# Projection products per head step: from a fixed rate to a rate worked out from what is left

## The chip, the cores and the metric

The kernel runs on one NeuronCore of a Trainium2 chip. The metric is the device time of one execution in microseconds (us), lower is better. The engines that matter are TensorE (PE: matmuls; PEld: its weight loads), VectorE (DVE), ScalarE (ACT), GpSimd (POOL), and SyncE (SP), which here only issues DMAs.

## The reference

A network of four layers on one sequence of 2048 rows by 640 columns. Layers 1 and 3 are attention in a sliding window, layers 2 and 4 a Fourier mixing:

```python
x = A_x
x = x + _A_ref(_layernorm(x, axis=-1), A_wqkv, A_wo)
x = x + _B_ref(_layernorm(x, axis=-1), B_dft_seq_re, ...)
x = x + _A_ref(_layernorm(x, axis=-1), A_wqkv, A_wo)
x = x + _B_ref(_layernorm(x, axis=-1), B_dft_seq_re, ...)
# _A_ref: qkv = x @ wqkv; 32 heads of 20 columns; a row attends to itself and the
# 255 rows before it (mask, softmax); the heads' outputs @ wo
# _B_ref: a, b = x @ dft_hid_re.T, x @ dft_hid_im.T; y = dft_seq_re @ a - dft_seq_im @ b
```

All of it is float32. The kernel keeps that accuracy by splitting every factor into a high and a low part and making three products of each.

## The kernel before, in words

The sequence is cut into 16 blocks of 128 rows (and 4 blocks `sb` of 512), the 32 heads into 8 quads of four. Only the attention layers are touched by the change. Each of them has a head loop (`heads`), written in the order in which the engines will run it; nothing reorders it afterwards.

The loop goes over `step` from -10 to 128. A step handles one block of rows of one quad: step t = 16 * quad + block. It holds two halves (`z` is 0 or 1), and for each half TensorE makes two score tiles of the block that stands ten steps ahead (`s_head`, L631), from which VectorE takes masked row maxima (L636), and two transposed score tiles of the block at hand (`t_pair`, L659), which ScalarE turns into exponentials (L669) and GpSimd masks (L675, L679). At the end of the step stand the 12 times 4 products with the values (`pv`, L694). Every fourth step the maxima are turned into rows (`m_rows`, L644, L647) and sent by two small DMAs into an extra row of the queries (L649, `qp<-mt`), which the transposed score tiles four steps later read.

Beside the heads, three kinds of other work are laid into the steps, always right behind the first half (and behind the second one too in steps before -1):

- **The projection** of queries and keys (`project`, `pieces`, `lockstep`, L257): 600 products in all, 15 for each 128 columns (`c`, ten of them) and each `sb`. One product is two matmuls on the two halves of the rows. 120 are done before the loop. Two blocks `sb` make a piece of 30 products, in two halves of 15; at its end ScalarE copies two banks out (L544), GpSimd cuts them in two parts (L552, L211) and SP stores them (L524, `qk_d<-c`, 512 KB each). From there they come back in the layout of the heads (`pack`, L594, 80 KB each, twelve for one quad and one `sb`, three to a step).
- **The output's first part** (`partials`): 16 units of 18 products (three of the five chunks of the heads' outputs times `wo`), also on L257 with 320 columns. They need all 600 projection products done, the chunks loaded and scaled (`load_o`, L859, L865, L892), and the rows of x, which are loaded four ahead (`load_y`, L952, `big<-x`, 320 KB each; added in by VectorE on L978). `prepare(0)`, `prepare(2)` and `prepare(4)` start these loads when the projection comes to its last column block, to the second half of it, and to its end.
- **The output's last part** (`late`), from step 127.

How many products a step gets is `nf`. `fill(nf)` takes the half of 15 that is under way and cuts what is left of it into equal shares near `nf`. The deadlines `due` can raise `nf`; neither in this kernel nor in the changed one do they. With the fixed rate the steps from 0 on have 4, 4, 4 and 3 products in turn, steps -2 and -1 have 10 and 5, and the 600 are done at step 91. Steps 92 to 96 have no such product. The output's first part begins at step 97 with 9 products a step. SP issues all DMAs in program order, and each waits until the DMA eight places before it has landed, since there are eight completion semaphores in turn.

Of the kernel before, what the change touches and what calls it, by code (L numbers as in the profile page):

```python
# [31 lines left out]
EARLY = 3  # L32
AHEAD_X = 4
AFTER = 4
RATE = 4
FIRST = 7
LATE = 9
BACK = 2
# [26 lines left out]
class Net:  # L65
# [540 lines left out]
    def heads(self, xsrc, xdst, hook):  # L606
# [116 lines left out]
        total = NCH * NSB * per_piece  # L723
        done = [2 * NSB * per_piece]
# [52 lines left out]
        for step in range(-LEAD, steps + 1):  # L777
# [10 lines left out]
            s, t, v = step + LEAD, step, step - 1  # L788
# [8 lines left out]
            if v >= 0 and v % 4 == 3:  # L797
                load_v(v // 4 + 2)
            if done[0] < total:
                nf = max([FIRST if t < -2 else RATE + (t < 0)]  # L800
                         + [(d - done[0]) / max(1, at - s) for at, d, _, _ in due])
            else:
                nf = LATE
# [1062 lines left out]
```

## Time and profile before

| | us |
|---|---|
| median of 3 executions | 2182.82 |
| lowest, highest | 2181.66, 2192.8 |
| the profiled execution | 2187.93 |
| its span, first to last instruction | 2186.2 |
| steps 0 to 95 of the first attention (160.8 to 424.0) | 263.2 |
| steps 96 to 127 of the first attention (424.0 to 529.2) | 105.2 |
| steps 0 to 95 of the second attention (1252.1 to 1514.6) | 262.5 |
| steps 96 to 127 of the second attention (1514.6 to 1618.2) | 103.6 |

A step's start is the start of its first L659 matmul, of which there are four in a step. All times in the text count from the span's start. In the chain of waits a row has a start, a length, and the work that the end of the span hung on at that time; "x8" is eight instructions. In the table of stretches a row has the length and then for each engine its busy time and the number of its instructions, the granted TensorE clock (1.00 is full), the share of the DMA engines and GB/s.

### The profile page before, as it was taken

What the parts mean: (1) busy time and instruction counts of PE and PEld (TensorE: products, weight loads), DVE (VectorE), ACT (ScalarE), POOL (GpSimd) and SP (SyncE); (2) the same over time, 40 slices, a digit from 0 to 9 for tenths busy, and PEclk for the clock granted to TensorE, in tenths of its full rate; (3) what the DMA queues carried; (4) which work ended last, traced back from release to release, by engine and by line L of the source; (5) the groups of instructions that cost most, each with busy time, mean ns of one, the idle gap of its engine ahead of it and who ended that gap; (6) DMA issues with size and microseconds to landing.
All of it is one profiled execution on the core that took longest, in us unless ns stands there. A gap on an engine that the chain in (4) does not pass through costs nothing.

```text
span 2186.2 us, 48927 instructions
## 1 busy us (share of the span) xinstructions
PE 2118.1 (97%) x17872; PEld 1783.2 (82%) x17872; DVE 1603.7 (73%) x3931; ACT 1140.5 (52%) x2125; POOL 958.0 (44%) x1562
## 2 busy tenths in 40 slices
PE   7999999988999999999999999999899999999999
PEld 7987777677878888889999877776778888888899
DVE  6358888886897868786661588888767968677676
ACT  3117777656554545452341177777565645445332
POOL 3037776765614222322430377767655033231324
PEclk9999999999999999999999999999999999999999
DMA  5546666785555354656645556567855454546653
GB/s 183 175 157 190 198 180 215 211 224 169 202 192 189 127 183 141 214 177 207 207 156 167 162 186 200 181 212 226 216 161 182 140 182 132 174 152 208 222 165 125
DMA packets 227089, 398.40 MB, mean 182 GB/s; under 512 B 39969, under 2 KB 86561, under 8 KB 226849
## 3 DMA queue, kind: packets, MB, share of 16 engines
q1 hardware_dynamic: 226848, 395.28, 57.3%
q8 instruction: 141, 2.31, 0.5%
q14 instruction: 100, 0.81, 0.1%
HBM read 273.94 MB, written 120.06 MB: 180 GB/s over the span
## 4 chain that ended last, share of the span: by engine, by line
PE 78%; DVE 7%; DMA 5%; ACT 4%; issue 3%; POOL 2%; SPq 1%; ACTq 0%; DVEq 0%; POOLq 0%
PE banks L1416 29%; PE banks L239 15%; PE banks L257 12%; PE banks L694 6%; PE banks L659 5%; PE banks L1704 5%; PE banks L631 5%; DMA qp<-qk_d 2%; DVE banks L636 1%; ACT pt L669 1%; DMA x_d<-x 1%; PE banks L341 1%; DMA kp<-qk_d 1%; ACT big L1039 1%; DVE qp L232 1%
## 5 line engine op out<-in xcount | busy, mean ns | idle before, releaser
L636 DVE CUSTOM_DVE_ANT_0 banks<-banks,mask 128x384 f32<-128x384 f32 (+2 forms) x1024 | 527.6, 557 | 123.0 <-PE banks L631 99.9
L669 ACT ACTIVATE pt<-banks 128x768 f32<-128x768 f32 (+2 forms) x512 | 393.8, 772 | 168.7 <-PE banks L659 55.2
L675 POOL TENSOR_SCALAR_AFFINE_SELECT pt<-pt 128x256 f32<-128x256 f32 x512 | 213.3, 417 | 213.8 <-ACT pt L669 192.0
L257 PE MATMUL banks<-big,wc 64*128 64x512 f32 x1920 | 271.1, 394 | 0.4 <-DVE pt L442 0.4
L659 PE MATMUL banks<-qp,kp 61*128 61x384 f32 (+2 forms) x1024 | 210.2, 381 | 22.8 <-DVE mc L636 17.4
L694 PE MATMUL banks<-pt,vq 128*32 128x128 f32 x5760 | 211.6, 278 | 3.5 <-ACT pt L669 3.4
L631 PE MATMUL banks<-kp,qp 60*128 60x384 f32 (+2 forms) x1024 | 205.5, 347 | 6.7 <-DVE mc L636 3.1
L257 PEld LDWEIGHTS banks<-big,wc 64*128 64x128 f32 x1920 | 186.8, 185 | 22.6 <-ACT x L544 1.5
L679 POOL TENSOR_SCALAR_AFFINE_SELECT pt<-pt 128x256 f32<-128x256 f32 x448 | 193.8, 433 | 0.0
L226 ACT ACTIVATE qp<-pt 128x512 fp32r<-128x512 f32 (+1 forms) x200 | 123.2, 625 | 128.1 <-DVE pt L1347 51.7
L232 DVE TENSOR_TENSOR qp<-pt,qp 128x512 fp32r<-128x512 f32 (+1 forms) x198 | 156.6, 798 | 42.1 <-ACT qp L226 40.5
L694 PEld LDWEIGHTS banks<-pt,vq 128*32 128x32 f32 x5760 | 142.4, 110 | 51.5 <-issue 35.3
L659 PEld LDWEIGHTS banks<-qp,kp 61*128 61x128 f32 x1024 | 108.0, 184 | 87.3 <-DVE mc L636 65.2
L1416 PE MATMUL banks<-qp,big 128*128 128x512 f32 x648 | 152.9, 390 | 0.0
L631 PEld LDWEIGHTS banks<-kp,qp 60*128 60x128 f32 x1024 | 123.6, 186 | 31.9 <-DVE mc L636 16.4
L1345 POOL TENSOR_TENSOR pt<-pt,pt 128x512 f32<-128x512 f32 x32 | 47.2, 1475 | 231.4 <-DMA pt<-c 173.4
L226 ACT ACTIVATE c<-pt 128x512 fp32r<-128x512 f32 x146 | 90.4, 625 | 111.1 <-POOL pt L1325 57.1
L636 DVE DVE_READ_ACCUMULATOR2_ANT mc<- 128x1 f32 x1024 | 145.0, 142 | 0.0
L1416 PEld LDWEIGHTS banks<-qp,big 128*128 128x128 f32 x648 | 120.8, 188 | 24.2
L232 DVE TENSOR_TENSOR c<-pt,c 128x512 fp32r<-128x512 f32 x144 | 113.8, 793 | 26.9 <-ACT c L226 24.4
L1416 PE MATMUL banks<-qp,xc 128*128 128x512 f32 x480 | 117.4, 391 | 4.3 <-DVE xc L232 2.8
L552 POOL CAST c<-x 128x512 fp32r<-128x512 f32 x64 | 38.9, 611 | 166.5 <-ACT x L544 162.3
(253 smaller groups left out, 4479.9 us busy)
## 6 DMA issues: line engine op xcount, KB each, us to landing
pt<-c SPq DMA_DIRECT2D x166, 512.0 KB
qk_d<-c SPq DMA_DIRECT2D x80, 512.0 KB
kp<-qk_d SPq DMA_DIRECT2D x384, 80.0 KB
qp<-qk_d SPq DMA_DIRECT2D x384, 80.0 KB
kp<-u_d SPq DMA_DIRECT2D x32, 640.0 KB
o_d<-ou SPq DMA_DIRECT2D x64, 256.0 KB
x_d<-x SPq DMA_DIRECT2D x48, 320.0 KB
v_d<-pt SPq DMA_DIRECT2D x16, 768.0 KB
```

Source lines behind the costliest of these rows:

```text
L226: nc.scalar.activation(hi, src, AF.Copy, scale=-1.0 if neg else 1.0)
L232: (eng or nc.vector).tensor_tensor(out=lo, in0=src, in1=hi.bitcast(F32), op=OP.subtract)
L239: self.nc.tensor.matmul(p, x, y, start=n == 0, stop=n == last)
L257: self.nc.tensor.matmul(ps[a], x[r], y[r], start=half + i == 0, stop=half == 1 and i == n - 1, skip_group_check=True)
L631: nc.tensor.matmul(p, qp[quad % 2][b:b + 60, z, qb * P:(qb + 1) * P], kp[quad % 2][b:b + 60, z, k0 * P:(qb + 1) * P], start=True, stop=True)
L636: nc.vector.tensor_tensor_reduce(out=p, in0=p, in1=self.mask[:, 384 - n * P:], scale=1.0, scalar=NEG, op0=OP.add, op1=OP.max, accum_out=mc ...
L659: nc.tensor.matmul(self.banks[:, banks[e], :n * P], kp[quad % 2][b:b + 61, z, kb * P:(kb + 1) * P], qp[quad % 2][b:b + 61, z, kb * P:(kb + ...
L669: nc.scalar.activation(pt[quad, kb][:, 2 * z:2 * z + 2, :n * P], self.banks[:, b0:b1 + 1, :n * P], AF.Exp, scale=SCALE)
L675: nc.gpsimd.affine_select(out=t[:, :, 0:P], in_=t[:, :, 0:P], pattern=[[0, 2], [1, P]], compare_op=OP.is_ge, fill=0.0, base=0, channel_mul ...
L679: nc.gpsimd.affine_select(out=t[:, :, 256:384], in_=t[:, :, 256:384], pattern=[[0, 2], [-1, P]], compare_op=OP.is_gt, fill=0.0, base=0, ch ...
L694: nc.tensor.matmul(self.banks[32 * h:32 * h + 32, bank, :P], vq[:, 96 * (kb % 4) + 21 * h:96 * (kb % 4) + 21 * h + 32], t[:, h, (qb - kb) ...
L1416: nc.tensor.matmul(self.banks[:, bk, :], p, b[q], start=start and m == 0, stop=stop and last and m == 2, skip_group_check=True)
```

## The change

The constant 4 goes. From step -2 on, the number of products is what is left of the 600 divided by the number of steps left until step 96; in the steps before -2 it stays 7.

```diff
-RATE = 4
+ROWS_AT = 96
...
             if done[0] < total:
-                nf = max([FIRST if t < -2 else RATE + (t < 0)]
+                nf = max([FIRST if t < -2 else (total - done[0]) / max(1, ROWS_AT - t)]
                          + [(d - done[0]) / max(1, at - s) for at, d, _, _ in due])
             else:
                 nf = LATE
```

What comes of it: the rate is 3.67 at step -2 and falls slowly. Steps -2 and -1 have 8 and 4 products (10 and 5 before). From step 0 to 72 the shares are 3, 4, 4, 4 in turn, that is the old row one step later. Steps 73 to 77, 82 to 86 and 91 to 95 have 3 each, and the 600 are done at step 95. The output's first part begins at step 97 as before. In steps 0 to 91 nine products fewer are made than before, in steps -2 and -1 three fewer, and twelve stand in steps 92 to 95.

TensorE at step 92, before. The two score pairs of the step stand with nothing between them; `pt` holds the exponentials, `vq` the values:

```order
L659 MATMUL banks<-qp_105,kp_104 128x384 x2
L631 MATMUL banks<-kp_561,qp_106 128x384 x2
L659 MATMUL banks<-qp_105,kp_104 128x384 x2
L631 MATMUL banks<-kp_561,qp_106 128x384 x2
L694 MATMUL banks<-pt_96,vq_93 32x128 x4
```

The same step in the changed kernel; `big_512` and `big_732` hold two blocks of the normalized rows, `wc` the weights:

```order
L659 MATMUL banks<-qp_105,kp_104 128x384 x2
L631 MATMUL banks<-kp_561,qp_106 128x384 x2
L257 MATMUL banks<-big_512,wc 128x512
L257 MATMUL banks<-big_732,wc 128x512
L257 MATMUL banks<-big_512,wc 128x512
L257 MATMUL banks<-big_732,wc 128x512
L257 MATMUL banks<-big_512,wc 128x512
L257 MATMUL banks<-big_732,wc 128x512
L659 MATMUL banks<-qp_105,kp_104 128x384 x2
L631 MATMUL banks<-kp_561,qp_106 128x384 x2
L694 MATMUL banks<-pt_96,vq_93 32x128 x4
```

Three products, six matmuls, now stand between the halves of steps 92 to 95.

SP from step 92 to 96, before:

```order
L621 DMA vq_92<-v_d 128x384
L952 DMA big_5880<-x 128x640 x2
L594 DMA qp_106<-qk_d 20x2x512 x3
L524 DMA qk_d<-c 128x2x512
L711 DMA sm<-ou_99 128x1x16
L712 DMA o_d<-ou_99 128x512
L717 DMA r_d<-rc 128x16
L952 DMA big_5880<-x 128x640 x2
L524 DMA qk_d<-c 128x2x512
L649 DMA qp_106<-mt 2x4x128 x2
L594 DMA kp_104<-qk_d 20x2x512 x3
```

The same stretch in the changed kernel:

```order
L621 DMA vq_92<-v_d 128x384
L594 DMA qp_106<-qk_d 20x2x512 x3
L711 DMA sm<-ou_99 128x1x16
L712 DMA o_d<-ou_99 128x512
L717 DMA r_d<-rc 128x16
L649 DMA qp_106<-mt 2x4x128 x2
L594 DMA kp_104<-qk_d 20x2x512 x3
L621 DMA vq_93<-v_d 128x384
L952 DMA big_6021<-x 128x640 x2
L594 DMA kp_104<-qk_d 20x2x512 x3
L952 DMA big_6021<-x 128x640
```

Four loads of x rows and the two last stores of the projection no longer stand ahead of the small L649 of step 95; the first of the loads follow in step 96.

SP in steps 98 and 99, before:

```order
L717 DMA r_d<-rc 128x16
L594 DMA qp_105<-qk_d 20x2x512 x3
L859 DMA x<-o_d 128x1x512
L865 DMA rr_101<-r_d 128x1x512
L649 DMA qp_106<-mt 2x4x128 x2
L594 DMA qp_105<-qk_d 20x2x512 x3
L952 DMA big_5880<-x 128x640
```

The same two steps in the changed kernel:

```order
L717 DMA r_d<-rc 128x16
L952 DMA big_6021<-x 128x640
L594 DMA qp_105<-qk_d 20x2x512 x3
L859 DMA x<-o_d 128x1x512
L865 DMA rr_101<-r_d 128x1x512
L524 DMA qk_d<-c 128x2x512
L952 DMA big_6021<-x 128x640
L649 DMA qp_106<-mt 2x4x128 x2
L594 DMA qp_105<-qk_d 20x2x512 x3
L952 DMA big_6021<-x 128x640
L524 DMA qk_d<-c 128x2x512
```

Here two of the loads and one store have come in ahead of the L649 and the last L594 of step 99, and a store behind them.

## The prediction

> **What bounds the kernel now.** I read the page's engine shares first, then the table of stretches over the two attentions, then the chain of waits inside a stretch, and last SP's timeline.
>
> ```profile
> span 2186.2 us, 48927 instructions
> PE 2118.1 (97%) x17872; PEld 1783.2 (82%) x17872; DVE 1603.7 (73%) x3931; ACT 1140.5 (52%) x2125; POOL 958.0 (44%) x1562
> ```
>
> ```profile
> 160.80:424.00 263.20, 257.55 (x3620) 194.44 (x3618) 219.59 (x821) 190.71 (x349) 194.27 (x443) 1.00 0.64 196
> 424.00:529.20 105.20, 94.11 (x1442) 76.55 (x1442) 73.50 (x230) 64.59 (x117) 66.56 (x143) 0.98 0.72 204
> 1252.10:1514.60 262.50, 256.80 (x3624) 193.72 (x3620) 219.19 (x820) 190.77 (x349) 194.43 (x443) 1.00 0.63 199
> 1514.60:1618.20 103.60, 92.92 (x1442) 75.34 (x1442) 74.64 (x232) 64.79 (x117) 66.45 (x143) 1.00 0.73 197
> ```
>
> TensorE is busy for 98% of steps 0 to 95 and VectorE for 83%: TensorE leads, but VectorE is close behind. The two attentions differ by 0.7 us up to step 96 and by 1.6 us after it. The chain inside the plain part of the loop (steps 57 to 72 of the first attention):
>
> ```profile
> 313.85 0.37 PE banks L659
> ...
> 316.50 0.37 PE banks L659 x2
> 316.87 0.18 PE banks L631 x2
> 317.05 0.93 PE banks L257 x8
> 317.97 0.17 PE banks L659 x2
> 318.14 0.17 PE banks L631 x2
> 318.32 0.79 PE banks L694 x24
> ...
> 321.06 0.21 PE banks L644
> ...
> 322.06 0.37 PE banks L659 x2
> ...
> 322.61 0.70 PE banks L257 x6
> ...
> 324.66 0.37 PE banks L659 x2
> ...
> 333.16 0.26 PE banks L659 x2
> ...
> 335.60 0.38 PE banks L659 x2
> ...
> 343.47 0.37 PE banks L659 x2
> ...
> 346.04 0.37 PE banks L659 x2
> ...
> 354.69 0.38 PE banks L659 x2
> ...
> 357.28 0.37 PE banks L659 x2
> ```
>
> The step at 316.50 is pure TensorE: 0.37 + 0.18 + 0.93 + 0.17 + 0.17 + 0.79 = 2.61 us with four products. Four cost 0.93 and three 0.70, so a product costs 0.23 us of TensorE. Without products a step would need 1.68 us of TensorE, with three 2.38; every fourth step has the 0.21 of L644 on top. The four three-product steps in these rows (322.06 to 324.66, 333.16 to 335.60, 343.47 to 346.04, 354.69 to 357.28) last 2.60, 2.44, 2.57 and 2.59, on average 2.55, which is 0.17 above TensorE's own 2.38: something else holds them. All sixteen steps last 357.28 - 313.85 = 43.43; the twelve with four products take 33.23, or 2.77 each, and 2.70 without the L644 of four of them. So going from four products to three has been worth 0.15, not 0.23.
>
> **Where no product stands.** The chain in steps 92 to 95, and in the table of stretches step 95, step 96 and the same four steps of the second attention:
>
> ```profile
> 413.00 0.37 PE banks L659 x2
> ...
> 413.60 0.56 DVE banks L636
> ...
> 420.88 0.26 PE banks L659 x2
> ...
> 424.07 0.62 PE banks L659 x2
> ...
> 428.09 3.85 DMA qp<-mt
> ```
>
> ```profile
> 420.88:424.07 3.19, 2.86 (x35) 1.84 (x34) 2.46 (x10) 1.14 (x4) 2.12 (x4) 0.72 0.99 349
> 424.07:427.86 3.79, 3.39 (x35) 2.11 (x34) 2.81 (x10) 2.20 (x4) 2.01 (x4) 0.50 0.66 206
> 1504.30:1514.60 10.30, 9.07 (x135) 6.00 (x131) 9.13 (x34) 6.36 (x15) 9.99 (x22) 1.00 0.79 251
> ```
>
> Steps 92 to 94 (413.00 to 420.88) last 2.63 each on average though TensorE needs about 1.68: the chain runs through VectorE's mask (0.56), behind which the next score pair waits. In the second attention the four steps last 10.30, or 2.58 each. So a step costs about 2.6 whether it holds no product or three, and TensorE has some 0.7 us of room for products in each of these four.
>
> **The change, part by part**, for one attention.
>
> *A. Three products fewer in steps -2 and -1.* Five products took 1.15 there, and at step 0 VectorE is behind:
>
> ```profile
> 156.55 1.15 PE banks L257 x10
> ...
> 161.61 0.46 DVE banks L636
> 162.07 0.06 DVE mc L636
> ```
>
> Three at 0.23 are 0.7 us at most. But in step 0 the chain passes to VectorE, where a mask costs 0.46 + 0.06 = 0.52 in a row; a half with two masks and their start is near the half with four products (0.18 + 0.93), so TensorE soon waits for VectorE. Ends: -0.7 and 0. I take -0.5, nearer to the TensorE row, since only step 0 shows the wait.
>
> *B. Steps 0 to 91: nine steps go from four products to three.* Ends: 9 x 0.23 = -2.1 if TensorE alone counts, 0 if a step's floor is 2.7 already. I take the difference seen in the quoted steps, 9 x 0.15 = -1.4. Up to step 72 the row 4, 4, 4, 3 is only moved by one step against the heads' own work. ScalarE's copies at the end of a piece still fall into a step of three products, as before, so I cost the shift at nothing; what hides it is that light step. If that cover were gone, a copy more or less in the way would be a few tenths in each of eleven pieces, 1 to 2 us either way.
>
> *C. Steps 92 to 95: twelve products come in.* With three, TensorE needs 2.38 (2.59 with L644 in step 94); the three-product steps seen last 2.55. Four of them with L644 once, and shorter score tiles in the last two, come to 10.2 to 10.4, against 10.30 in the second attention: 0. Ends: +2.8 (12 x 0.23, nothing hidden) and -0.4 (if the wait for the mask disappears behind the products). In the steps from 96 on the last two bank copies, the GpSimd cuts and the two stores come later by four steps; these steps hold nine products, and ScalarE is busy there for 64.79 of 103.60 and GpSimd for 66.45, so I cost their engine time at nothing.
>
> *D. The clock.* In the first attention the granted clock falls to 0.72 in step 95 and 0.50 in step 96, at the end of the steps without products. In the second it stays at 1.00. By the first table this attention loses 0.7 up to step 96 and 1.6 behind it, together 2.3. With products in steps 92 to 95 I expect no fall: -2 in this execution, ends -2.3 and 0. Whether the executions behind the median had the fall isn't shown, so I count half of it there, -1. The page "TensorE: Matmul & The Clock Gate" of the Trainium skill says, under "HAM oscillation — how this bites in real kernels", that TensorE falls to half clock after idle gaps over about 3.4 us. By that rule these steps, with gaps under 1 us, should not have lost the clock, and the sum would be without this term, 1 us higher. The row of 0.50 differs from the page, and the row decides.
>
> *E. SP and the DMAs around steps 95 to 102.* SP's timeline and, last, the chain in the second attention:
>
> ```profile
> 1514.37 0.80 SPq L952 DMA_DIRECT2D big<-x_d  x2
> 1515.27 0.38 SPq L524 DMA_DIRECT2D qk_d<-c  x1
> ...
> 1517.45 1.19 SPq L594 DMA_DIRECT2D kp<-qk_d  x3
> ...
> 1531.11 1.26 SPq L594 DMA_DIRECT2D qp<-qk_d  x3
> ```
>
> ```profile
> 1532.02 4.17 DMA qp<-qk_d
> ```
>
> Step 102 begins quad 7's scores and can't start before the last L594 of step 99 has landed, at 1536.19, 21.6 us after step 96 began. Between 1517.45 and the last issue of that group at 1532.02 SP issues 24 DMAs, 0.6 us each, without a pause worth naming. In the changed kernel SP reaches step 96 earlier, since two loads and a store (1514.37 to 1515.65, some 1.3 us, and the waits around them) are gone from ahead of it; but five more stand between there and step 99's last L594: 5 x 0.6 = 3.0. Net +1.7 on SP, and by bytes (4 x 0.32 + 0.5 = 1.8 MB at the 251 GB/s of the row quoted above is 7.2 us, less the 1.15 MB, 4.6 us, of two loads and a store that were in flight at 1515 anyway) +2.6. Against it the L649 of step 95 is freed of the loads ahead of it: the 3.85 us wait of the first attention shrinks. Ends: -1.3 and +5. I take +1.0 an attention.
>
> The sum: A -0.5, B -1.4, C 0, E +1.0 make -0.9 an attention, -1.8 for both, and D -2: -3.8 from the profiled execution's own 2187.9, that is 2184.1. The median of the runs stands 5.1 below that execution, so from 2182.8, with half of D, 2182.8 - 2.8 = 2180.0.
>
> **The rivals.**
>
> *R1, slower: the loads in a bunch hold up SP.* Each DMA waits for the one eight places back. Six loads of x rows (four moved, two that were there) and two stores now stand in steps 96 to 99. For it: SP has no room there, and the one L524 issued at 1515.27 is of the kind that lands late under load. Against it: the bytes up to step 102 are the same. Its price: the upper end of E, 5 us an attention, instead of +1: 2180 + 8 = 2188, and 2192 if A and B give nothing as well. It decides where the first load of x rows, issued in the second half of step 96, lands later than VectorE needs it, which is at the end of step 98, some 8 us on: then L978 blocks the masks behind it.
>
> *R2, faster: TensorE alone counts.* A and B in full, -2.8 an attention, C -0.4, E -1.3 because the waits at steps 97 and 98 go: -4.5, twice, and -2 for the clock: 2182.8 - 11 = 2172. For it: 98% busy, and the step of 2.61 that is pure TensorE. Against it: three-product steps have not come below 2.44.
>
> *R3, nothing: the floor of the step.* If a three-product step in a run of them lasts as long as a four-product one, A to E cancel and only the clock may differ: 2182, between 2181 and 2184. For it: 2.6 with none and 2.55 with three.
>
> *R4: the clock falls elsewhere.* If the wait at step 102 grows by 1 us, TensorE idles over 5 us there, and a fall as in D costs 2.3 an attention: 2180 + 4.6 = 2185. For it: the fall in the first attention. Against it: the 4.17 us wait left the second attention's stretch at 1.00. [...]
>
> **How the numbers follow.** Forecast 0.42 (2176 to 2183), R3 0.22, R1 0.16, R2 0.14, R4 0.06. The predicted time is the forecast's, 2180. Range: down to 2170, just below R2's 2172, and up to 2193, R1 with nothing from A and B; what is left out is the tails of R1 and R2, about 0.15. 0.5% is 10.9 us, about what a measurement of this kernel can tell from no change: faster means under 2171.9, slower above 2193.7. R2 lies at the lower bound and gives 0.12 with a tail of the forecast; R1 reaches the upper with its tail, and with an alignment of steps 0 to 72 worse by 0.06 a step (6 us an attention), 0.14. The rest, 0.74, is within.
>
> **What would show it.** Right: steps 92 to 95 at 10.2 to 10.4 us with six L257 matmuls each and a clock of 1.00; steps 0 to 91 shorter by 1 to 2 us an attention; three-product steps at about 2.55; the DMA wait at step 102 a little longer, the wait for qp<-mt near step 97 gone. Wrong: a mean step other than 2.7 in steps 0 to 72 (the shift is not free), L978 waiting for big<-x at step 98, or SP late by more than 3 us at step 99.

## The result and the profile after

The changed kernel takes 2182.91 us in the median of 20 executions (2178.11 to 2187.48), the kernel before, run beside it, 2188.73 in the median of 20 (2181.66 to 2195.65). The ratio over the executions is 0.9981, with a 95% interval of 0.9972 to 0.9989, which is about 4 us; the two medians are 5.8 us apart. So the changed kernel is 4 to 6 us faster, a fifth to a quarter of a per cent. The 2182.82 shown before the prediction was the median of three executions and stood at the low end of the twenty.

The page of the changed kernel, its span and the engine shares, and its table of stretches: the two attentions (steps 0 to 95, then 96 to 127), steps 0 to 72 and 73 to 91 of the first, steps 92 to 95 of both, and 3 us inside step 102. Columns as before: length, then busy time of TensorE, weight loads, VectorE, ScalarE and GpSimd, granted clock, DMA share, GB/s.

```profile
span 2183.4 us, 48970 instructions
PE 2119.3 (97%) x17872; PEld 1785.2 (82%) x17872; DVE 1602.8 (73%) x3931; ACT 1139.6 (52%) x2125; POOL 961.1 (44%) x1562
...
159.70:419.60 259.90, 256.65 (x3628) 195.26 (x3624) 220.18 (x821) 190.41 (x349) 191.16 (x438) 1.00 0.65 197
419.60:525.80 106.20, 94.27 (x1442) 76.70 (x1439) 73.78 (x232) 64.80 (x118) 70.39 (x150) 0.98 0.71 206
1246.90:1507.00 260.10, 256.85 (x3628) 195.07 (x3625) 220.18 (x821) 190.38 (x349) 191.15 (x438) 1.00 0.64 197
1507.00:1615.40 108.40, 96.76 (x1442) 78.21 (x1442) 74.25 (x232) 64.89 (x118) 70.45 (x150) 0.96 0.72 197
...
159.72:356.88 197.16, 194.84 (x2758) 149.46 (x2757) 166.16 (x625) 144.23 (x263) 143.32 (x333) 1.00 0.64 195
356.88:408.45 51.57, 50.66 (x720) 37.84 (x717) 44.42 (x163) 38.34 (x69) 37.87 (x86) 1.00 0.68 209
408.40:419.60 11.20, 11.17 (x159) 7.95 (x153) 9.63 (x35) 7.85 (x17) 10.00 (x21) 1.00 0.72 198
1495.70:1507.00 11.30, 11.27 (x160) 8.00 (x155) 9.68 (x35) 7.90 (x17) 10.05 (x21) 1.00 0.60 179
442.10:445.10 3.00, 2.96 (x22) 2.96 (x23) 0.36 (x2) 0.00 (x0) 0.83 (x2) 0.50 0.77 260
```

The same view of the kernel before, for steps 0 to 72 and 73 to 91 of the first attention:

```profile
160.79:359.86 199.07, 195.66 (x2760) 148.77 (x2758) 164.94 (x624) 144.44 (x263) 142.66 (x331) 1.00 0.63 194
359.86:412.93 53.07, 52.06 (x735) 39.27 (x731) 45.05 (x164) 39.80 (x74) 41.56 (x91) 1.00 0.66 203
```

Steps 0 to 95 became shorter by 3.3 and 2.4 us (263.2 to 259.9, 262.5 to 260.1), steps 96 to 127 longer by 1.0 and 4.8. Of the gain in the first attention, 1.9 us lie in steps 0 to 72, which hold one product fewer (two matmuls in the counts), and 1.5 in steps 73 to 91, which hold eight fewer. Steps 92 to 95 cost 11.2 us in both attentions.

The chain of waits through steps 98 to 103 of the first attention, after the change (start, length, what the end hung on):

```profile
427.86 0.81 DVE big L978
...
436.53 0.44 SPq L594
437.02 0.36 SPq L594
437.42 4.68 DMA qp<-qk_d
442.14 0.47 PE banks L631
442.61 2.51 PE banks L257 x18
...
447.04 1.33 PE banks L257 x18
```

The wait that ended the chain at step 102 before ends it still: the last L594 lands at 442.10, 22.5 us after step 96 began. Right behind it 18 matmuls take 2.51 us, and the same 18 in the next step 1.33: the granted clock was 0.50 in those 3 us, as the last stretch above shows. The second attention has the same fall at the same place.

For all kernels of this case the stretches, from the starts of the steps in each profiled execution, first / second attention, in us ("lead" is the first L631 of the head loop to step 0):

| kernel | lead | 0-72 | 73-91 | 92-95 | 96-99 | 100-103 | 104-127 |
|---|---|---|---|---|---|---|---|
| before | 35.8 / 35.2 | 199.1 / 199.0 | 53.1 / 53.2 | 11.1 / 10.3 | 14.6 / 12.5 | 14.2 / 15.3 | 76.3 / 75.7 |
| after | 35.1 / 34.5 | 197.2 / 197.3 | 51.6 / 51.6 | 11.2 / 11.2 | 12.7 / 12.7 | 17.5 / 17.5 | 76.1 / 78.3 |
| e1_shift | 35.1 / 34.5 | 197.1 / 197.3 | 52.1 / 52.1 | 10.3 / 10.6 | 13.5 / 11.9 | 16.3 / 19.5 | 76.5 / 76.5 |
| e2_tail | 35.8 / 35.2 | 199.1 / 198.9 | 51.3 / 51.1 | 11.2 / 11.3 | 12.6 / 12.6 | 15.7 / 19.6 | 82.7 / 76.9 |
| e3_light1 | 35.1 / 34.5 | 196.2 / 196.9 | 52.3 / 52.3 | 10.7 / 10.8 | 12.2 / 12.2 | 14.6 / 17.1 | 78.3 / 78.4 |
| e4_light2 | 37.1 / 36.4 | 197.6 / 197.8 | 53.3 / 53.3 | 10.2 / 10.3 | 13.9 / 15.7 | 13.1 / 13.1 | 76.2 / 78.2 |
| e5_rows92 | 35.2 / 34.5 | 197.3 / 196.9 | 52.3 / 52.3 | 10.5 / 10.5 | 12.6 / 12.8 | 18.8 / 18.9 | 76.9 / 78.5 |
| e6_ahead2 | 35.1 / 34.5 | 197.0 / 197.8 | 51.6 / 51.5 | 11.3 / 11.2 | 12.6 / 12.6 | 13.9 / 16.1 | 77.6 / 75.7 |
| e7_pack_early | 35.1 / 34.5 | 197.2 / 197.2 | 51.5 / 51.6 | 11.2 / 11.2 | 13.0 / 13.5 | 14.7 / 13.7 | 79.9 / 75.9 |
| e8_early_light1 | 37.3 / 36.7 | 198.3 / 198.0 | 53.2 / 53.1 | 10.3 / 10.3 | 12.6 / 13.2 | 13.7 / 14.5 | 76.9 / 75.8 |
| e9_cut1 | 35.8 / 35.2 | 197.1 / 197.2 | 53.1 / 53.2 | 11.0 / 10.3 | 13.9 / 13.4 | 13.8 / 16.5 | 77.4 / 75.8 |
| e10_cutback | 35.1 / 34.5 | 197.4 / 197.7 | 51.7 / 51.7 | 11.2 / 11.2 | 12.7 / 12.6 | 17.9 / 19.0 | 76.4 / 75.8 |
| e11_both | 35.1 / 34.5 | 197.1 / 197.1 | 51.6 / 51.5 | 11.2 / 11.2 | 15.8 / 12.6 | 13.1 / 13.0 | 78.8 / 78.4 |
| e12_light1_both | 35.1 / 34.5 | 196.1 / 196.2 | 52.3 / 52.5 | 10.7 / 10.7 | 14.4 / 12.1 | 12.9 / 12.9 | 76.6 / 76.8 |

The columns up to step 95 repeat between the two attentions of an execution within 0.8 us, most within 0.3. Those behind it scatter by 1 to 6 us, since a fall of the clock there comes in one execution and not in the next. So the experiments are read by their stretches first, and by their times where several executions were taken. The letters that name theories in the expectations hold within a group of runs.

### The profile page after: what moved, and what is told of

The parts are those of the page before. It is cut to its first block, busy times and chain, and to the rows that moved or that the text cites. A ratio compares the mean times of both kernels' runs of the same rounds, so it can differ in the third digit from the quotient of the medians.

```text
span 2183.4 us, 48970 instructions
## 1 busy us (share of the span) xinstructions
PE 2119.3 (97%) x17872; PEld 1785.2 (82%) x17872; DVE 1602.8 (73%) x3931; ACT 1139.6 (52%) x2125; POOL 961.1 (44%) x1562
## 4 chain that ended last, share of the span: by engine, by line
PE 79%; DVE 7%; DMA 5%; ACT 4%; issue 3%; POOL 2%; SPq 1%; ACTq 0%; DVEq 0%; POOLq 0%
PE banks L1416 29%; PE banks L239 14%; PE banks L257 13%; PE banks L694 7%; PE banks L659 6%; PE banks L631 5%; PE banks L1704 5%; DVE banks L636 1%; DMA kp<-qk_d 1%; DMA kp<-u_d 1%; DVE qp L232 1%; ACT pt L669 1%; PE banks L341 1%; ACT big L1039 1%; POOL rs L1087 1%
## 5 line engine op out<-in xcount | busy, mean ns | idle before, releaser
L636 DVE CUSTOM_DVE_ANT_0 banks<-banks,mask 128x384 f32<-128x384 f32 (+2 forms) x1024 | 527.0, 556 | 116.7 <-PE banks L631 98.9
L659 PE MATMUL banks<-qp,kp 61*128 61x384 f32 (+2 forms) x1024 | 210.1, 380 | 21.5 <-DVE mc L636 16.4
L631 PE MATMUL banks<-kp,qp 60*128 60x384 f32 (+2 forms) x1024 | 210.2, 350 | 4.9 <-DMA qp<-qk_d 3.5
L226 ACT ACTIVATE qp<-pt 128x512 fp32r<-128x512 f32 (+1 forms) x200 | 123.2, 625 | 129.0 <-DVE pt L1347 52.1
L659 PEld LDWEIGHTS banks<-qp,kp 61*128 61x128 f32 x1024 | 108.4, 185 | 85.3 <-DVE mc L636 62.3
L631 PEld LDWEIGHTS banks<-kp,qp 60*128 60x128 f32 x1024 | 126.7, 186 | 29.6 <-DVE mc L636 16.0
L636 DVE DVE_READ_ACCUMULATOR2_ANT mc<- 128x1 f32 x1024 | 143.6, 140 | 0.0
```

What stands on the lines that cost most here:

```text
L226: nc.scalar.activation(hi, src, AF.Copy, scale=-1.0 if neg else 1.0)
L631: nc.tensor.matmul(p, qp[quad % 2][b:b + 60, z, qb * P:(qb + 1) * P], kp[quad % 2][b:b + 60, z, k0 * P:(qb + 1) * P], start=True, stop=True)
L636: nc.vector.tensor_tensor_reduce(out=p, in0=p, in1=self.mask[:, 384 - n * P:], scale=1.0, scalar=NEG, op0=OP.add, op1=OP.max, accum_out=mc ...
L659: nc.tensor.matmul(self.banks[:, banks[e], :n * P], kp[quad % 2][b:b + 61, z, kb * P:(kb + 1) * P], qp[quad % 2][b:b + 61, z, kb * P:(kb + ...
```

## The experiments

### Which part of the change gains

The shift of the row 4, 4, 4, 3 alone, from the kernel before:

```diff
-                nf = max([FIRST if t < -2 else RATE + (t < 0)]
+                nf = max([FIRST if t < -2 else RATE]
```

> The kernel before with four products from step -2 on (8 and 4 in steps -2 and -1 instead of 10 and 5), so that the row 4, 4, 4, 3 becomes 3, 4, 4, 4 one step later, as in the changed kernel up to step 72, and the projection ends at step 92. Theory S (the shift against the heads' own work brings the gain of steps 0 to 72): steps 0 to 72 last 197.2 us as in the changed kernel, not 199.0, and the start of the heads is 0.7 earlier; steps 73 to 91 keep before's 53.1 within 1 us. Rival N (only the number of products counts; one fewer in steps 0 to 72): 198.8 in steps 0 to 72. In all S gives about 4 us off, N about 1.5.

The rest of the change without the shift, from the changed kernel:

```diff
-                nf = max([FIRST if t < -2 else (total - done[0]) / max(1, ROWS_AT - t)]
+                nf = max([FIRST if t < -2 else 4 + (t < 0) if t < 72 else (total - done[0]) / max(1, ROWS_AT - t)]
```

> The kernel before up to step 71 (10 and 5, then 4, 4, 4, 3), and from step 72 on what is left divided by the steps left until step 96, three products in most steps, so that the projection ends at step 95 without the shift. Theory S: steps 0 to 72 stay at 199.0 us; steps 73 to 91 last 51.6 as in the changed kernel (53.1 before), the four steps after it 10.3 to 11.2, step 102 waits as in the changed kernel (+2 us in steps 100 to 103). In all 0 to 3 us off. Rival N: the same stretch carries the gain, and steps 0 to 72 of the changed kernel were a matter of that run: 197.3 here too.

Measured: the shift alone 2181.84 us, ratio to before 0.9962 (0.9947 to 0.9976); the rest alone 2192.44, ratio 1.0018 (1.0008 to 1.0028). The product of the two is the 0.998 of the change. Steps 0 to 72 with the shift, and below it without, then step 110 of the first attention without it:

```profile
159.76:356.86 197.10, 194.78 (x2758) 149.21 (x2757) 166.31 (x625) 144.21 (x263) 143.30 (x333) 1.00 0.66 194
```

```profile
161.45:360.57 199.12, 195.72 (x2759) 148.41 (x2757) 165.07 (x624) 144.22 (x263) 142.69 (x332) 1.00 0.63 194
...
472.02:480.79 8.77, 5.98 (x55) 4.66 (x51) 3.57 (x11) 1.91 (x5) 3.64 (x7) 0.66 0.83 188
```

The shift gives the whole gain of steps 0 to 72. The stretching of the tail gains as well where it was meant to (73 to 91: 53.1 to 51.3), but loses more behind step 96, and comes out slower than before where 0 to 3 us less had been expected. So the two halves of this change have opposite signs. The smaller edit, which takes three products from ahead of step 0, has the better ratio, 0.9962 against 0.9981, though the two intervals touch.

### Where the light step stands

Two more places of the light step. One step later again, by five steps of three products (from the kernel before):

```diff
-                nf = max([FIRST if t < -2 else RATE + (t < 0)]
+                nf = max([FIRST if t < -2 else (3 if 33 <= t < 38 else RATE)]
```

> As e1_shift, but with five steps of three products from step 32 on, so that from step 37 on the light step of three products stands at t = 1 modulo 4 (before: 3; changed: 0). Steps 48 to 63 last 43.4 us before and 43.1 in the changed kernel. Theory S says that the place of the light step against the heads' work sets this: I expect 42.8 to 43.8, not the same as either within 0.1. Rival N: 43.2 within 0.15, whatever the place.

One step earlier, with seven products a fill in step -2:

```diff
-                nf = max([FIRST if t < -2 else RATE + (t < 0)]
+                nf = max([FIRST if t < -1 else RATE]
```

> The kernel before with seven products also in step -2 (8 and 7, then 4 a step), so that the light step stands at t = 2 modulo 4, where the rows of maxima are turned (L644), and the projection ends at step 90. Theory S: steps 48 to 63 differ from 43.4 by over 0.2 us; with the 0.21 us of L644 in the light step I expect the steps to be more even and the sixteen to last 42.7 to 43.2. Rival N: 43.4 within 0.15.

And the place of the first, reached by more products ahead of step 2 instead of fewer at step 33:

```diff
-                nf = max([FIRST if t < -2 else RATE + (t < 0)]
+                nf = max([FIRST if t < -1 else 5 if t < 2 else RATE]
```

> The kernel before with seven products also in step -2 and five in steps -1 to 1, then 4 a step: the light step stands at t = 1 modulo 4 (the best place seen, 42.8 us for sixteen steps) and the projection ends at step 89. Theories S and L together: sixteen steps 42.8, steps 0 to 91 at 249 to 250 in spite of three products more in them than in e3_light1, steps 100 to 103 at 13 to 14 us with the clock at 1.00. In all 2172 to 2178, the fastest so far. Rival: the early end takes back what the shift brings (steps 90 to 96 without products still cost 2.6 each), and it ends at 2180 to 2184.

Measured: 2180.63 us (one execution), 2188.09 (one) and 2185.08 (ten, ratio 0.9989, 0.9976 to 1.0002). The first did a little better than the changed kernel in steps 0 to 72; here are these steps and, below, steps 48 to 63 alone:

```profile
160.01:356.22 196.21, 194.19 (x2753) 147.68 (x2752) 166.60 (x624) 144.14 (x263) 143.26 (x332) 1.00 0.64 193
289.29:332.18 42.89, 42.63 (x616) 32.42 (x613) 36.47 (x137) 31.48 (x58) 30.87 (x74) 1.00 0.63 193
```

The second took 43.2 and 43.1 us for steps 48 to 63, at the upper end of what was expected; it gained nothing in the first half of a quad and paid 1.3 us more in the lead. The third missed what was expected of it, 2172 to 2178, and its interval doesn't tell it from the kernel before: its light step stood at the same place of four as in the first, but steps 48 to 63 took 43.2 us, not 42.9. So the place among four steps is not the variable. By steps of sixteen, which is one quad and also one block of weights (60 products), the medians of the steps show more:

| step in the quad | 2 | 4 | 5 | 6 | 10 | 12 | 13 | 14 | steps 0-7 | steps 8-15 |
|---|---|---|---|---|---|---|---|---|---|---|
| before | 2.63 | 2.91 | 2.97 | 2.78 | 2.95 | 2.85 | 2.61 | 3.03 | 21.7 | 21.7 |
| after | 2.75 | 2.60 | 2.88 | 2.75 | 2.95 | 2.60 | 2.87 | 2.86 | 21.4 | 21.7 |
| e3_light1, from step 40 | 2.75 | 2.62 | 2.60 | 2.96 | 2.86 | 2.62 | 2.59 | 3.02 | 21.4 | 21.5 |
| e4_light2 | 2.56 | 3.02 | 2.62 | 2.69 | 2.80 | 2.62 | 2.62 | 2.76 | 21.8 | 21.4 |

A step without a stall lasts about 2.60, whether it has three products or four (2.43 to 2.49 in the last step of a quad, whose transposed tiles have 128 columns). The change took 0.3 us out of the first half of each quad and next to nothing out of the second.

### What the shift removes

In the first half of a quad VectorE cuts the next block of weights, in two subtractions (L211 into `wc`). In the kernel before it meets them in step 5, between row maxima over 384 columns (VectorE's timeline, step 53 of the first attention; start, length):

```profile
305.57 0.25 DVE L714 RECIPROCAL rc<-sm 128x16 f32<-128x16 f32 x1
305.74 0.58 DVE L211 TENSOR_TENSOR wc<-x,wc 128x384 fp32r<-128x384 f32 x1
306.24 0.55 DVE L636 CUSTOM_DVE_ANT_0 banks<-banks,mask 128x384 f32<-128x384 f32 x1
...
307.23 0.54 DVE L211 TENSOR_TENSOR wc<-x,wc 128x256 fp32r<-128x256 f32 x1
307.70 0.55 DVE L636 CUSTOM_DVE_ANT_0 banks<-banks,mask 128x384 f32<-128x384 f32 x1
```

From 305.06 to 308.17 VectorE goes without a pause through four maxima, the reciprocal and two cuts, 3.1 us where a step has 2.6. Step 54 is the one in which the score tiles of the next quad begin, with 128 columns and maxima of 0.3 us. After the shift the cuts fall there. To see whether it is this and not the bank copies or GpSimd's cuts of the projected rows, which the shift moves as well, the weight cut alone was moved, from the kernel before by one step:

```diff
-                    self.cut_chunk(c + 1)
+                    self.cut_chunk(c + 1) if lead else self.post(2, lambda c=c: self.cut_chunk(c + 1))
```

> The kernel before, with one thing moved: the cut of the next block of weights (ScalarE's L219, VectorE's L211 into wc, 0.58 and 0.54 us, once in 16 steps) is asked for one step later, so that VectorE finds it between masks of 128 columns (0.3 us each) and no longer between masks of 384 (0.55 each). Products, copies, stores and loads stay where they are. Theory V (what the shift removes is VectorE's queue behind this cut): steps 16 to 23, 32 to 39, 48 to 55 and 64 to 71 go from 21.7 to 21.4 us, the other eights stay, steps 0 to 72 last 197.5 to 198.0 (199.0 before, 197.2 after the change), and the time is 2 to 4 us below the kernel before. Theory S (it is ScalarE's bank copies or GpSimd's cuts of the projected rows, which move with the products): steps 0 to 72 stay at 198.8 to 199.2 and the time is that of the kernel before.

And in the changed kernel by three steps, to maxima over 384 columns again:

```diff
-                    self.cut_chunk(c + 1)
+                    self.cut_chunk(c + 1) if lead else self.post(6, lambda c=c: self.cut_chunk(c + 1))
```

> The changed kernel, with the same weight cut asked for three steps later: VectorE meets it again between masks of 384 columns, beside a reciprocal, as in the kernel before. Theory V: the eights 8 to 15, 24 to 31, 40 to 47, 56 to 63 go from 21.7 to 21.9 to 22.1, steps 0 to 72 from 197.2 to 198.3 to 198.9, and the time is 2 to 3 us above the changed kernel's 2182.9. Theory S: steps 0 to 72 stay at 197.0 to 197.4 and the time at 2183.

Measured: 2184.78 us (ten executions, ratio 0.998, 0.9966 to 0.9994), and 2183.59 (ten, ratio 0.9972, 0.9962 to 0.9983). VectorE's timeline and steps 0 to 72 in the first of the two:

```profile
307.29 0.74 DVE L211 TENSOR_TENSOR wc<-x,wc 128x384 fp32r<-128x384 f32 x1
307.95 0.29 DVE L636 CUSTOM_DVE_ANT_0 banks<-banks,mask 128x128 f32<-128x128 f32 x1
...
308.41 0.88 DVE L211 TENSOR_TENSOR wc<-x,wc 128x256 fp32r<-128x256 f32 x1
309.21 0.28 DVE L636 CUSTOM_DVE_ANT_0 banks<-banks,mask 128x128 f32<-128x128 f32 x1
...
160.89:358.03 197.14, 194.84 (x2760) 148.93 (x2758) 166.99 (x624) 144.43 (x263) 143.16 (x331) 1.00 0.64 196
```

GpSimd and SP have their work in the old order, and TensorE its products in the old steps; only the cut moves, VectorE's two subtractions and, ahead of them, ScalarE's two copies of the high part (L219), which belong to it. Steps 0 to 72 fall from 199.1 to 197.1, as far as with the shift. Step 5 of the quad goes from 2.97 to 2.63 and the others stay; steps 16 to 23 go from 21.65 to 21.34, steps 24 to 31 from 21.85 to 21.73. So the place of the cut alone is enough for the whole gain of these steps.

TensorE shows who held it. In the kernel before, its first L659 of steps 22, 38, 54 and 70 begins after 0.22 to 0.23 us without a matmul, in both attentions; with the cut moved, it begins after none in all eight. Five of the eight waits are put down to VectorE's L636. The other three, step 54 of the first attention among them, are put down to a load (L594) that lands at the same moment; but the loads stand in the same order in both kernels, and the wait is as long where none lands.

The other kernels fit. Where the light step comes earlier, the cuts come earlier: in step 4 of e4_light2 and step 3 of e8_early_light1 they stand between maxima over 384 columns, and these steps last 3.02 and 2.99, which fits the miss of the latter. Step 6 of the changed kernel, where they stand between maxima over 128, lasts 2.75. The step ahead of the cuts is long in each of these kernels as well, 2.91, 3.02, 2.97 and 2.88; it moves with the row, and what holds it isn't settled.

The run also shows that the busy time was no guide: VectorE is busy for 2 us more (164.94 to 166.99), because the cuts take longer at their new place, and the kernel is shorter.

The reverse fell short of what was expected: steps 0 to 72 went from 197.2 to 197.4 and 197.3 to 197.7, not to 198.3 or more, and the time did not rise. Steps 8 to 15 of a quad took 21.82, 0.1 us more and not 0.2 to 0.4. The ten subtractions of steps 0 to 72 in the kernel before, in the changed one, and with the cut three steps later (min/median/max in ns):

```profile
L211 DVE TENSOR_TENSOR wc<-x,wc x10: 543/562/764, 174.9 to 350.7; 128x384 fp32r<-128x384 f32 x5, 128x256 fp32r<-128x256 f32 x5
```

```profile
L211 DVE TENSOR_TENSOR wc<-x,wc x10: 722/730/764, 176.4 to 350.2; 128x384 fp32r<-128x384 f32 x5, 128x256 fp32r<-128x256 f32 x5
```

```profile
L211 DVE TENSOR_TENSOR wc<-x,wc x10: 451/476/496, 184.4 to 358.6; 128x384 fp32r<-128x384 f32 x5, 128x256 fp32r<-128x256 f32 x5
```

At that place the cuts are shorter by 0.09 each, and the light step stands right ahead of theirs (56 and 57, where before it was 51 and 53). That may be why it costs less there; it wasn't separated. So taking the cut away is shown to be enough for the gain, and putting it back between wide maxima is not shown to undo it. One cut in the changed kernel, and one with the cut three steps later, each with GpSimd's masks beside it:

```profile
306.03 0.75 DVE L211 TENSOR_TENSOR wc<-x,wc 128x384 fp32r<-128x384 f32 x1
...
305.96 0.41 POOL L675 TENSOR_SCALAR_AFFINE_SELECT pt<-pt 128x256 f32<-128x256 f32 x1
306.32 0.72 POOL L679 TENSOR_SCALAR_AFFINE_SELECT pt<-pt 128x256 f32<-128x256 f32 x1
```

```profile
313.99 0.49 DVE L211 TENSOR_TENSOR wc<-x,wc 128x384 fp32r<-128x384 f32 x1
...
313.99 0.76 POOL L679 TENSOR_SCALAR_AFFINE_SELECT pt<-pt 128x256 f32<-128x256 f32 x1
```

A cut that begins just behind the start of a mask takes 0.75 us; one that begins with it takes 0.49, and then the mask takes 0.76 instead of 0.41. In the kernel before, the changed one and the one with the cut moved by one step, each of the thirty subtractions of steps 0 to 72 of the first attention lasts 0.41 us (384 columns) or 0.28 us (256) plus what was left, when it began, of the GpSimd instruction then running, within 0.01. The Trainium skill, page "SBUF — State Buffer", section "Who interferes with whom", says that a VectorE instruction with two SBUF inputs contends with a GpSimd instruction that reads SBUF, and that the order in which they start decides which of them waits. The trace agrees.

Steps 73 to 91 point the same way. There the shift alone, with 72 products against 71 before, took 52.1 us in place of 53.1; the changed kernel, with 63, took 51.6. So 1.0 of the 1.5 gained there comes with the shift and not with fewer products. The longest of these steps before is step 85, 3.64 us, in which VectorE cuts the output's weights between maxima over 384 columns:

```profile
394.54 0.94 DVE L211 TENSOR_TENSOR big<-we,big 128x640 fp32r<-128x640 f32 x1
395.40 0.55 DVE L636 CUSTOM_DVE_ANT_0 banks<-banks,mask 128x384 f32<-128x384 f32 x1
```

With the shift alone these cuts begin one step later, and no step of the stretch lasts over 3.12. They were not moved by themselves, so here the cause is argued only.

### The end of the projection and SP

The projection done by step 92 instead of 96, otherwise as changed:

```diff
-ROWS_AT = 96
+ROWS_AT = 92
```

> The changed kernel with 92 in place of 96: the shift stays, but the projection ends at step 91 as before, so the loads of x rows and the last two stores stand in steps 92 to 95 again. Theory L (the late end of the projection costs in steps 96 to 103, through SP and the DMAs): steps 100 to 103 last 14.2 to 15.3 us as before, not 17.5; steps 0 to 91 last 249.5 (after: 248.8, before: 252.1); in all 2 to 4 us less than the changed kernel. Rival: the long step 102 came with the shift or was a matter of the run, and steps 100 to 103 stay at 17 us.

Two of x's row blocks loaded ahead instead of four, which takes two loads off SP before step 102:

```diff
-AHEAD_X = 4
+AHEAD_X = 2
```

> The changed kernel with two loads of x rows started ahead instead of four, so that two fewer DMAs (0.64 MB) stand ahead of the last L594 of step 99. Theory L, by SP's 0.6 us a DMA and 251 GB/s: this L594 lands 1.2 to 2.5 us earlier (22.5 us after step 96 began in the changed kernel), steps 100 to 103 last 14.5 to 16 us, and with less idle time TensorE keeps its clock there. Rival: the stores and the loads of the heads' outputs set it, and step 102 stays at 6.5 us. If x rows come too late, L978 waits in steps 98 to 102 instead.

The first group of the last quad's rows sent two steps earlier:

```diff
-        due = [(16 * q + 4 * j - AHEAD + 2 * (q == NQ - 1),
+        due = [(16 * q + 4 * j - AHEAD + 2 * (q == NQ - 1 and j > 0),
```

> The changed kernel with the first twelve copies for quad 7 (L594) two steps earlier, in steps 94 to 97 instead of 96 to 99, ahead of most of the loads of x rows. Theory L: step 102 no longer waits for them (3.4 us instead of 6.5), steps 100 to 103 last 13 to 14 us, and the granted clock stays at 1.00 there, so 3.5 to 4.5 us an attention come back, if nothing else is late next (the rows of maxima, L649, of step 99). Rival: another wait takes its place in steps 98 to 104 and less than 1.5 us an attention come back.

Measured: 2184.61 us (ten, ratio 0.9978, 0.9965 to 0.9991), 2180.6 (one) and 2178.55 (one). With the end at 92, step 102 of both attentions, and the chain in the first:

```profile
443.08:450.49 7.41, 5.80 (x52) 4.57 (x53) 2.06 (x9) 1.62 (x2) 2.51 (x7) 0.58 0.87 209
1531.83:1539.54 7.71, 5.70 (x52) 4.56 (x52) 2.05 (x9) 1.62 (x2) 2.37 (x7) 0.59 0.85 222
...
440.81 4.53 DMA qp<-qk_d
```

Steps 100 to 103 took 18.8 and 18.9, where 14.2 to 15.3 had been expected of an earlier end. The wait of 4.53 us is there with the early end as well, and the clock fell behind it, so a late end is not the cause alone. Two loads fewer made these steps 13.9 and 16.1. With the rows sent earlier (the second attention's step 102, then the first attention's step 110 and what the chain shows there):

```profile
1528.34:1531.55 3.21, 3.21 (x52) 2.72 (x52) 1.75 (x8) 1.81 (x3) 2.30 (x6) 1.00 0.97 325
...
468.18:475.66 7.48, 5.15 (x56) 4.04 (x53) 3.50 (x11) 1.92 (x5) 3.40 (x7) 0.77 0.74 191
...
467.62 1.68 SPq L952
...
469.74 3.68 DMA kp<-qk_d
473.44 4.18 DMA o_d<-ou
```

Step 102 needs 3.21 us when its rows are there, against 6.5 in the changed kernel (439.99 to 446.47 by its steps). So the end of steps 100 to 103 is set by when SP gets to the last L594 and by its landing. What is gained there is lost again in part eight steps later, where the next rows are late in turn (7.48, against 3.93 in the changed kernel).

### Both edits on SP, and the best of the rest

The two edits above together, on the changed kernel:

```diff
-AHEAD_X = 4
+AHEAD_X = 2
...
-        due = [(16 * q + 4 * j - AHEAD + 2 * (q == NQ - 1),
+        due = [(16 * q + 4 * j - AHEAD + 2 * (q == NQ - 1 and j > 0),
```

> The changed kernel with x rows loaded two ahead instead of four and the first group of the last quad's rows sent two steps earlier: both edits of the two runs before on SP. Theory L (SP and the landing of its loads set steps 100 to 111): steps 100 to 103 at 13.0 to 13.6 in both attentions, no clock fall there, steps 104 to 111 at 28 to 30, time 2174 to 2178. If the wait is only passed on to step 110: steps 104 to 111 at 30 to 32 and the time 2178 to 2181.

And on the kernel with the five steps of three products (from the kernel before):

```diff
-AHEAD_X = 4
+AHEAD_X = 2
...
-        due = [(16 * q + 4 * j - AHEAD + 2 * (q == NQ - 1),
+        due = [(16 * q + 4 * j - AHEAD + 2 * (q == NQ - 1 and j > 0),
...
-                nf = max([FIRST if t < -2 else RATE + (t < 0)]
+                nf = max([FIRST if t < -2 else (3 if 33 <= t < 38 else RATE)]
```

> The kernel before without the extra product in steps -2 and -1, with three products a step in steps 33 to 37 (the row of 4, 4, 4, 3 stands one step later again from there on), and the two edits on SP of the run above. The projection ends at step 93. Steps 0 to 72 at 196.2 to 196.9 as in the run with that row alone, steps 92 to 95 at 10.7, steps 100 to 103 at 13 to 14. By theory V and L together 2172 to 2177; if the two edits give nothing beyond a shorter step 102, 2177 to 2181.

Measured: 2175.93 us (six executions, 2173.25 to 2181.11), ratio to before 0.9941 (0.9926 to 0.9956), and 2176.33 (six, 2173.25 to 2181.3), ratio 0.994 (0.9925 to 0.9955). Both are where they were expected, both beat the kernel before and the changed one. Steps 100 to 103 of both attentions in the first and in the second of them:

```profile
435.96:449.01 13.05, 12.44 (x205) 10.54 (x201) 9.74 (x37) 8.82 (x16) 9.62 (x21) 0.99 0.89 268
1520.14:1533.15 13.01, 12.39 (x206) 10.49 (x203) 10.20 (x39) 8.86 (x17) 10.32 (x22) 1.00 0.89 285
```

```profile
432.60:445.50 12.90, 12.39 (x203) 10.46 (x203) 9.54 (x38) 8.06 (x15) 8.51 (x20) 1.00 0.90 249
1513.93:1526.83 12.90, 12.40 (x202) 10.46 (x203) 9.54 (x38) 8.06 (x15) 8.53 (x20) 1.00 0.84 230
```

These four steps come to 13 us, 4.5 less than in the changed kernel and 1.2 to 2.3 less than before. Step 110 of the second attention still waits in the first of them (4.86). Which of the two is better the six executions don't tell.

## Why the prediction was right, and where it wasn't

The time forecast was 2180.0, within 2170 to 2193, and "within 0.5%" held the largest chance; 2182.91 is in the range and the ratio within 0.5%. The forecast put the change 2.8 us below the kernel before, and the runs side by side put it 4 to 6 below. But the terms of the sum came out otherwise than written, and that the total is near is luck: for both attentions together B and C were to bring 2.8 us and steps 0 to 95 became 5.7 shorter; D and E were to cost 1.0 and steps 96 to 127 became 5.8 longer.

- **A** (three products fewer in steps -2 and -1, -0.5): the lead became shorter by 0.7 in both attentions (35.8 to 35.1, 35.2 to 34.5). Steps 0 to 7 shortened by another 0.2 beyond what the weight cut explains (22.21 and 22.16 with the cut alone moved, 21.96 and 22.01 after). Close to the end of -0.7, a little past it.
- **B** is the step that failed: "I cost the shift at nothing; what hides it is that light step". The prediction looked at the bank copies of ScalarE, and the light step did stand under them. What it did not look at is the other work laid against the same position: VectorE's cut of the next weights, which the shift moved from the widest row maxima to the narrowest. Steps 0 to 91 gained 3.3 us an attention, not 1.4: 1.7 to 1.9 in steps 0 to 72, where the cut alone gives 1.8 to 1.9, and 1.5 in steps 73 to 91 (53.1 to 51.6). These 1.5 over eight products are 0.19 each, near the 0.15 of the forecast, but a product has no such price: 1.0 of them came with the shift alone, and the nine products fewer from there to the changed kernel gave 0.5. Plain steps last 2.60 with three products or four, and the gain is in fewer long steps (in steps 80 to 91 of the first attention those above 2.76 were 2.91, 3.64, 2.99, 2.90, 3.16, and are 2.81, 3.38, 3.18, 2.80). The three-product steps were forecast at 2.55 and last 2.60 (steps 82 to 86: 2.56, 2.58, 2.60, 2.59, 2.68). One of the four that made up the 2.55, the 2.44, was the last step of a quad with its 128 columns; the other three average 2.59, so the floor of 2.6 was there to be read.
- **C** (twelve products into steps 92 to 95, at nothing, 10.2 to 10.4): mis-sized. They last 11.2 and 11.2 (2.90, 2.96, 2.87 and 2.43 in the first), 0.9 more than the 10.3 of before in the second attention. With the end at step 91 (e5_rows92) they are 10.5, with the end at 93 (e12_light1_both) 10.7. The clock is at 1.00 as forecast. What holds these steps above 2.6 isn't settled: TensorE's chain has its score matmuls waiting there, and GpSimd is busy for 10.0 of 11.2.
- **D** (the fall of the clock at steps 95 and 96 goes, -1): it went, and steps 96 to 99 of the first attention came down from 14.6 to 12.7. But new falls came in step 102 of both attentions and at step 126 of the second, so the term as a sum is not there.
- **E** (SP and the DMAs, +1.0): the landing that opens step 102 went from 21.6 us after step 96 to 22.5, as forecast; the last L594 was issued 17.8 us after it (437.42), before 17.4 (1532.02 after 1514.6). In the second attention of the changed kernel it is 22.7 and 18.2. The wait for qp<-mt near step 97 is gone. What the term left out is the fall behind the longer wait.

Of the rivals, R1 did not happen: SP was not late by 3 us at step 99, and L978 at 427.86 stands in the chain by its own work of 0.81 us, with a wait of 0.51 for TensorE ahead of it and none for a load. R2 is refuted by the long steps that remain. R3's premise, a floor of 2.6 for the step, is true of plain steps, and its time of 2182 is nearest to the absolute 2182.91; but its reading that nothing changes is not, by the interval and by the 3.3 us of steps 0 to 91. R4, given 0.06, came true in this execution: steps 100 to 103 took 17.5 in both attentions, 3.3 and 2.2 more than before, of which the later landing is 0.9 and the half clock some 1.2 for every 18 matmuls. Its condition was wrong, though. It took the load's 4.17 us for idle time of TensorE, which had other matmuls to do meanwhile: its longest stretch without one in that step was 2.05 us. Step 102 of the second attention in the kernel with only the weight cut moved, which has SP's order of before, and the same step before:

```profile
1530.52:1537.28 6.76, 4.93 (x55) 4.03 (x52) 2.49 (x11) 2.33 (x5) 3.18 (x7) 0.75 0.86 184
```

```profile
1533.57:1539.14 5.57, 3.52 (x56) 2.78 (x52) 2.28 (x10) 2.31 (x5) 2.94 (x7) 1.00 0.87 185
```

The longest stretch without a matmul was 1.83 us in the first, which lost the clock, and 2.05 in the second, which kept it, with SP's order the same in both. So the fall is not decided by one microsecond more of waiting.

That the median of three, 2182.82, was low against the later 2188.73 helped the absolute number: from 2188.7 the same sum would have said 2185.9.

## What to carry to other kernels

When a change moves a row of work by one step against another loop, look at everything that is laid out by that row's position, on every engine, and at what each piece meets at its new place; here the place of a cut of about 1 us, once in sixteen steps, was worth 1.8 to 1.9 us an attention, where nothing had been forecast. An engine that is busy for 83% on average can be the bound in one step of sixteen, and that step is found by the median length of each step over the period, not by the busy time. A change that stretches work to fill free room pushes its stores and loads into the next stage: test its halves apart, since they may have opposite signs, and follow the DMA queue behind it.

## What the runs showed of the hardware

The granted clock falls in pieces of one size: but for the one at the very end, every fall in these traces lasted 3.4 or 6.8 us at 0.50, and an execution had two to ten such pieces of 3.4. The Trainium skill, page "TensorE: Matmul & The Clock Gate", section "What's actually happening", gives a free-running window of 3413 ns; the lengths agree with it. That TensorE has to idle for a whole such time, as the section of the Trainium skill named in the prediction has it, they don't show: apart from the two steps 102 just shown, it fell in step 95 of the first attention before, where no stretch without a matmul in the 6.8 us ahead of the fall was over 0.43 us. Which measure of TensorE's work decides it is not settled here. Half clock for 3.4 us is at most 1.7 us lost, so five pieces more or less make 8.5, about the 9 between the shortest and the longest execution of the changed kernel; that this is the cause of that scatter was not shown.

The other thing is the price of VectorE's subtraction with two inputs from SBUF: 476, 562, 730 or 838 ns in the median of the same ten instructions, their own time plus the rest of what GpSimd had running. The longest of these (838, with the cut alone moved) stood in a kernel that was faster than before.
